# Attention and a PEER expert block on one core: the output weights prepared in the fold, the maxima of v taken over steps 76 to 118, the first projection at step 73, and three loads asked for at other places

## The chip, the cores and the metric

The kernel runs on one core of one Trainium2 chip. The metric is the device time of one launch in microseconds (us). Three runs of the kernel before took 1602.69, 1601.28 and 1598.19 us, so the median is 1601.28 us.

## The reference

A block of 2048 tokens of 448 features with two halves, each behind a layer norm and added to its input: softmax attention with 16 heads of 28 features, and a PEER layer, which picks 8 of 4096 experts per token and head through two sets of 64 sub-keys.

```python
x = A_x
h = x + _A_ref(_layernorm(x), A_wqkv, A_wo)        # 16 heads of 28 features, softmax, times wo
h2 = h + _B_ref(_layernorm(h), B_w_q, B_k1, B_k2, B_u, B_v)
...
# _B_ref, for every token and each of 16 heads
q = einsum("nd,dhc->nhc", xf, w_q)                 # 2 x 256 per head
s1 = einsum("nhd,ed->nhe", q[..., :256], k1)       # 64 scores
s2 = einsum("nhd,ed->nhe", q[..., 256:], k2)       # 64 scores
# the 8 best of each, the 8 best of their 64 sums, softmax over these: g, expert numbers top_e
act = gelu(einsum("nd,nhkd->nhk", xf, u[top_e]))
out = einsum("nhk,nhk,nhkd->nd", g, act, v[top_e])
```

## The kernel before

**Splitting.** Most products run as float16: each operand is scaled by a power of two and split into a high and a low part, so a product takes 11 or 12 matmuls of 128 rows instead of 4. The scale comes from the largest magnitude of the whole weight (class `Scale`): `see` takes the maximum of a piece on VectorE (L157), `share` takes it over all pieces (L160), spreads it (L161, tile `every`), turns it on TensorE (L165, PSUM tile `M`) and sets the scale (L178 to L181). The weights u and v are each read twice: once for the maximum (`tops`, tile `seen`, 4 buffers, 32 pieces), once to be scaled and split on GpSimd (`part`, tiles `raw` and `hl`) and written back to DRAM.

**Stages.** First the queries, keys and values of all tokens are made and written to DRAM. Then attention runs as 256 steps, and everything else of this stage is woven around it. Step u works on one of 16 groups (a block of 512 tokens and 4 heads) and on one of 16 key tiles: the scores of step u+2 (L574, tile `S`), their exponential on ScalarE (L578, tile `P`), and the values of step u (L652, PSUM tile `A`, one buffer, copied to `on` by VectorE at L659 at the end of a group). For the steps in the set `paired` the values of two steps are computed in one go. `divide` then takes the row sums through DRAM (`sum`, `rec`, `rb`) and scales `on` over the next steps (L601, L610, L611).

**The fold, steps 0 to 67.** Beside attention, the query weights of 16 heads are multiplied with the sub-keys (`Fold.run`: L280, copies `wt`, transposes L291, copies `of`), scaled and split (`Fold.parts`) and written as four weights `wp`, one for each four heads. The maxima of u are taken in steps 1 to 45.

**Steps 68 to 256.** `load_wo` loads the output weights `wo` in steps 68 to 76, takes their maximum and splits them into `woh` and `wol`. For each of the first three token blocks a projection (`project`, 26 steps: copies `oh` and `ol`, 12 matmuls with `woh` and `wol`, layer norm, transposing DMA `Xb<-hl`) starts at `begin[b]`, and a search (`search`, 33 steps) follows it: 16 score tiles of 11 matmuls with the weights `w` (L100, `M<-w,Xb`), one `fresh` tile each, and the 8 best of each 64 on VectorE (L873, L875, tile `ti`). `pairs_of` then finds the best sums (`cand`, `ts`, `pos` on VectorE, `sel` on GpSimd). The maxima of v are taken in steps 112 to 156, and v is split from step 162.

**The order.** `weave` merges the generators by due times: an entry `(generator, n, lo, hi)` gets its n turns spread evenly between steps lo and hi. Each engine executes its own instructions in exactly this order and waits in it. All DMAs are issued by SyncE (SP) from one queue in program order: where one of them must wait (for the buffer that it overwrites, or for data), all later ones wait behind it.

**The loads.** A piece of keys and values (`kS`, `V`) serves four steps; there are 4 buffers of each. At its last step the buffer is asked to be refilled with the piece four further on (L241 and L229, `load_kv`). The fold's raw weights `wr` have 8 buffers (4 heads), refilled right behind the matmuls that read them (L267). The search's tiles `w` come from one pool of 3 buffers: high and low part for one group of four heads and the high part for the next; a score tile that is the last of its group uses the low weights first.

Of the kernel before, what the change touches and what calls it, by code (L numbers as in the profile page):

```python
# [64 lines left out]
def block(ctx: ExitStack, tc: tile.TileContext, x, wqk, wv, wo, wq, k12, uT, v, cst, out):  # L65
# [120 lines left out]
    def times(dst, src, c):  # L186
        nc.vector.tensor_scalar(dst, src, c, None, op0=OP.mult)
# [19 lines left out]
    def flush():  # L207

        while due:
            due.pop(0)()  # L210
# [40 lines left out]
    class Fold:  # L251
# [18 lines left out]
        def run(self, pool, psum):  # L270

            self.folded = {}
            for h in range(H):
                yield
                flush()
                pf = psum.tile([128, 512], F32, name="M")
                w = self.raw.pop(h)
                for kt in range(2):
                    for f in range(2):
                        nc.tensor.matmul(pf[64 * f:64 * f + 64, :D], self.keys[:, f, kt], w[f][:, kt],  # L280
                                         start=kt == 0, stop=kt == 1)
                wt = pool.tile([128, 512], F32, name="wt")
                due.append(lambda: (nc.vector.tensor_copy(wt[:, :D], pf[:, :D]),
                                    nc.vector.tensor_copy(wt[:, D:], pf[:, 384:D])))
                self.load(h + 4)
                yield
                yield
                flush()
                pt = psum.tile([128, 4, 128], F32, name="M")
                for t in range(4):  # L290
                    nc.tensor.transpose(pt[:, t], wt[:, 128 * t:128 * t + 128], ident)  # L291
                of = self.folded[h] = pool.tile([128, 512], F32, name="of", bufs=8)
                due.append(lambda: (nc.vector.tensor_copy(of, pt.rearrange("p t c -> p (t c)")),
                                    WS[h // 4].see(h % 4, of)))
                yield
# [265 lines left out]
    def attention(paired):  # L561
# [84 lines left out]
        def values(u, Pt):  # L646
            n, k = divmod(u, NT)
            if k == 0:
                O[n] = P[0].tile([128, 512], F32, name="A")
            V = kv[u // 4][1]  # L650
            for j in range(4):
                nc.tensor.matmul(O[n][32 * j:32 * j + 32], V[:, k % 4, j], Pt[:, j], start=k == 0, stop=k == NT - 1)  # L652
            if k % 4 == 3:
                load_kv(u // 4 + 4)
            if k == NT - 1:
                b, g = divmod(n, 4)
                if g == 0:
                    on[b] = (w2 if b % 2 else pp).tile([128, 4, 512], F32, name="on", bufs=1)
                nc.vector.tensor_copy(on[b][:, g], O.pop(n))  # L659
# [19 lines left out]
        yield  # L679


    def load_wo():
        S = Scale("o", 4)
        raw = w2.tile([128, 4, 512], F32, name="on", bufs=1).rearrange("p g c -> p (g c)")[:, :4 * D].rearrange("p (g c) -> p g c", c=D)
        nc.sync.dma_start(raw, wo)
        yield
        yield
        for g in range(4):
            S.see(g, raw[:, g])
        yield  # L690
        yield from S.share()
        nc.vector.tensor_scalar(hscale, hscale, S.floor, 2.0 ** -TOP, op0=OP.mult, op1=OP.mult)
        for g in range(4):
            times(woh[:, g], raw[:, g], S.scale)
            nc.vector.scalar_tensor_tensor(wol[:, g], raw[:, g], S.scale, woh[:, g], op0=OP.mult, op1=OP.subtract)
            yield

    WO = 9

    X = {}  # L700

# [129 lines left out]
    def search(b, order):  # L831


        loads = {}
        heads = [i for n, (i, j) in enumerate(order) if not n or order[n - 1][0] != i]

        def load(n, k):

            if n < len(heads):
                loads[n, k] = w = sp.tile([128, 4, 4, 128], F16, name="w", bufs=3)  # L840
                nc.sync.dma_start(w, wp_d[heads[n]][:, k])

        load(0, 0)
        load(0, 1)
        load(1, 0)
        yield
        last = None
        g = 0
        for n, (i, j) in enumerate(order):
            if last:  # L850
                best(*last)
            turned = n + 1 == len(order) or order[n + 1][0] != i
            src = sp.tile([128, 512], F32, name="fresh", bufs=2)
            nc.scalar.activation(src, scores_of(*X[b], (loads[g, 0], loads[g, 1]), j, turned), AF.Identity, scale=gscale[:, i:i + 1])  # L854
# [280 lines left out]
    with tc.manual_schedule(engines={ET.PE, ET.DVE, ET.Activation, ET.Pool, ET.SP}):  # L1135
        load_kv(2)
        load_kv(3)
        begin = [FOLDED + 8, 67 + 66, 69 + 128]
        a = attention({4 * h for h in range(1, H)} | {t + k for t in begin for k in (1, 7, 13, 19)}
                      | {t + 25 + 2 * n for t in begin for n in range(16)})  # L1140
        weave((islice(a, FOLDED), FOLDED, 0, FOLDED), (fold[0].run(fold_p, P[0]), Fold.STEPS, 0, Fold.STEPS),
              *[(fold[0].parts(fold_p, i), Fold.PARTS, 16 * i + (18 if i < 3 else 16), 16 * i + 32 if i < 3 else FOLDED) for i in range(4)],
              (tops(US, lambda f: uT[:, f].rearrange("p t e -> p (t e)"), 512), TOPS, 1, 45), (US.share(), 3, 47, 50),
              (parts_of_up(0, 7), 7 + PART, 51, FOLDED))
        fp.close()
        bx = ctx.enter_context(tc.tile_pool(name="bx", bufs=1, reuse_waits="tile"))
# [12 lines left out]
        bs = ctx.enter_context(tc.tile_pool(name="bs", bufs=1, reuse_waits="tile"))  # L1159
        spare = [bs.tile([128, 512], F32, name=f"ring{i}") for i in range(16, 18)]  # L1160
        r2 = ExitStack()
        wo_p = r2.enter_context(tc.tile_pool(name="wo_p", bufs=1, reuse_waits="tile"))
        w2 = r2.enter_context(tc.tile_pool(name="w2", bufs=2, reuse_waits="tile"))
        woh = wo_p.tile([128, 4, D], F16)
        wol = wo_p.tile([128, 4, D], F16)
        work = [(a, 257 - FOLDED, 0, 257 - FOLDED), (load_wo(), WO, 0, 8)]
        for b in range(3):
            t = begin[b] - FOLDED
            look = search(b, [(i, j) for g in ((0, 1), (2, 3)) for i in range(4) for j in g])
            work += [(project(b), PROJECT, t, t + PROJECT), (islice(look, 1), 1, t + 20, t + 21)]  # L1170
            t += 26
            p = 64 * b + 174 - FOLDED
            work += [(look, SEARCH, t, t + SEARCH)]
            if b < 2:
                work += [(chain(*[pairs_of(j, nc.gpsimd) for j in range(4)]), 4 * PAIRS_POOL, t + 18, p),
                         (places_of(b, nc.scalar), PLACES, p, p + 2 * PLACES)]
            else:
                work += [(pipeline([pairs_of(j, nc.gpsimd) for j in (0, 1)], 6), 6 + PAIRS_POOL, t + 20, 257 - FOLDED)]
        w0 = weights(0)

        def first_tokens():
            load_X(0)
            yield

        work += [(islice(w0, 1), 1, 220 - FOLDED, 221 - FOLDED), (first_tokens(), 1, 234 - FOLDED, 235 - FOLDED)]
        work += [(parts_of_up(7, 32), 25 + PART, 0, 90), (tops(VS, lambda f: v[:, f], D), TOPS, 44, 88), (VS.share(), 3, 89, 92), (scales(), 1, 93, 94),
                 (parts_of_down(0, 32), 32 + PART, 94, 186)]
        weave(*work)
    att.close()
# [192 lines left out]
```

## Time and profile before

| | |
|---|---|
| median of three runs | 1601.28 us |
| the profiled execution: its time | 1600.6 us |
| its span, from the first to the last instruction | 1598.8 us |
| attention with the fold (steps 0 to 67), about | 158 to 321 us |
| attention with projections and searches (steps 68 to 256), about | 321 to 840 us |
| experts | behind that, to the end |
| DMA | 270.36 MB, mean 169 GB/s |

The profile gives, per engine, the busy time, its share of the span and the instructions; the chain of waits that ended last; groups of instructions by line; and a timeline. TensorE is PE, its weight loads are PEld, VectorE is DVE, ScalarE is ACT, GpSimd is POOL, and SPq is SyncE issuing DMAs. `x12` behind a row is the number of merged instructions, and `[7.72 <-DMA on<-in_wo_dram]` says that the engine sat idle for 7.72 us before it, until that DMA had landed. In a table of stretches each engine has its busy time with the number of instructions behind it, and the last three columns are the clock granted to TensorE, the share of the DMA engines' time and GB/s.

### The profile page before, as it was taken

Reading aid. Unit: us, or ns where it says so; the run is one execution under the profiler, and the core shown is the slowest. Engines: PE = TensorE matmul, PEld = TensorE weight load, DVE = VectorE, ACT = ScalarE, POOL = GpSimd, SP = SyncE. Lnnn points to the kernel's source line nnn. Section 1 sums busy time; section 2 is a strip of 40 time slices with the busy share of each in tenths; the row PEclk is TensorE's granted clock in tenths of the full one; section 3 lists DMA queues with packets and bytes.
Section 4 is the critical chain, followed back from the end, with each engine's and each line's share of the span. In section 5 each row is a group of like instructions: output and inputs, shape, how many; then the busy total and the mean of one; then the engine's idle time right before and its main releaser. Section 6 shows DMA issues by size and latency. Waiting matters only on the chain.

```text
span 1598.8 us, 33145 instructions
## 1 busy us (share of the span) xinstructions
PE 1528.5 (96%) x12441; PEld 646.8 (40%) x12441; DVE 1169.8 (73%) x3944; ACT 908.4 (57%) x1220; POOL 361.2 (23%) x484
## 2 busy tenths in 40 slices
PE   5999999989999999999998999999999999999998
PEld 3444222222232233222334654455445554554444
DVE  8763355554378877766598899789998998889623
ACT  3544888878788788987874432344423343333321
POOL 1242000524315754797662000000000000000000
PEclk9999999999999999999999999999999999999999
DMA  8424787557786866678733344454344534443344
GB/s 279 137 99 129 229 267 251 184 163 204 220 252 214 243 209 221 189 203 255 256 114 106 98 133 129 129 180 118 106 135 129 158 104 146 129 135 114 120 143 133
DMA packets 176042, 270.36 MB, mean 169 GB/s; under 512 B 29900, under 2 KB 105932, under 8 KB 175880
## 3 DMA queue, kind: packets, MB, share of 16 engines
q1 hardware_dynamic: 171656, 266.14, 54.1%
q10 hardware_dynamic: 4224, 2.10, 0.5%
q8 instruction: 97, 1.59, 0.4%
q14 instruction: 65, 0.53, 0.1%
HBM read 215.91 MB, written 49.50 MB: 166 GB/s over the span
## 4 chain that ended last, share of the span: by engine, by line
PE 70%; DVE 21%; DMA 3%; POOL 2%; issue 2%; ACT 1%; SPq 1%; DVEq 0%; POOLq 0%
PE acc L1290 14%; PE A L652 12%; PE M L100 12%; PE S L574 11%; PE A L100 9%; PE pq L100 6%; DVE p L1051 4%; DVE G L1072 2%; DVE fg L1036 2%; PE M L280 2%; DVE f L1030 1%; DVE ring L1262 1%; DVE pos L875 1%; PE A L1078 1%; DVE w L1265 1%
## 5 line engine op out<-in xcount | busy, mean ns | idle before, releaser
L578 ACT ACTIVATE P<-S,escale 128x1024 f32<-128x1024 f32 x512 | 533.5, 1122 | 84.8 <-PE S L574 78.9
L1290 PE MATMUL acc<-v,w 128*128 128x448 f16 x1536 | 308.3, 354 | 1.3 <-DVE w L1265 1.0
L652 PE MATMUL A<-P,V 128*32 128x512 f32 x2048 | 259.7, 605 | 2.4 <-DVE on L659 2.4
L574 PE MATMUL S<-qS,kS 32*128 32x512 f16 x3072 | 237.2, 380 | 3.0 <-ACT P L578 2.2
L1290 PEld LDWEIGHTS <-w 128*128 128x128 f16 x1536 | 148.4, 98 | 143.5 <-DVE w L1265 4.0
L100 PEld LDWEIGHTS <-u 128*128 128x128 f16 x1386 | 131.4, 98 | 147.4 <-issue 8.5
L100 PE MATMUL A<-Xb,u 128*128 128x512 f16 x759 | 178.6, 384 | 2.5 <-DVE G L1072 2.5
L100 PE MATMUL M<-w,Xb 128*128 128x512 f16 x704 | 163.8, 380 | 9.8 <-DMA w<-wp 5.0
L1216 ACT ACTIVATE ring<-A,ugelu 128x512 f32<-128x512 f32 x71 | 48.7, 687 | 217.9 <-PE A L100 217.9
L1051 DVE TENSOR_TENSOR p<-st,iota 128x2048 f16<-128x2048 f16 x128 | 156.1, 1220 | 15.7 <-PE M L1068 8.1
L574 PEld LDWEIGHTS <-kS 32*128 32x128 f16 x3072 | 65.5, 92 | 214.5 <-issue 179.0
L1262 DVE SCALAR_TENSOR_TENSOR ring<-ring,wscale,G 128x512 f32<-128x512 f32 x128 | 92.1, 745 | 77.5 <-ACT ring L1216 77.4
L100 PE MATMUL M<-Xb,u 128*128 128x512 f16 x627 | 147.8, 382 | 0.0
L100 PEld LDWEIGHTS <-Xb 128*128 128x128 f16 x704 | 63.6, 97 | 99.7 <-issue 25.9
L873 DVE MAX8 ti<-fresh 128x8 f32<-128x64 f32 x384 | 57.0, 210 | 59.7 <-ACT fresh L854 59.6
L1264 ACT ACTIVATE w<-ring 128x512 f16<-128x512 f32 x128 | 75.9, 622 | 41.1 <-DVE ring L1262 28.6
L652 PEld LDWEIGHTS A<-P,V 128*32 128x32 f32 x2048 | 47.9, 109 | 126.2 <-issue 114.2
L1108 POOL TENSOR_SCALAR raw<-raw,scale 128x512 f32<-128x512 f32 (+1 forms) x64 | 47.2, 737 | 209.6 <-DVE r L601 145.4
L1265 DVE SCALAR_TENSOR_TENSOR w<-w,ring 128x512 f16<-128x512 f16 x128 | 84.9, 685 | 7.2 <-ACT w L1264 6.9
L1216 ACT ACTIVATE ring<-M,ugelu 128x512 f32<-128x512 f32 x57 | 39.2, 688 | 89.2 <-PE M L100 87.5
L1036 DVE TENSOR_TENSOR fg<-f,st 128x2048 f16<-128x2048 f16 x64 | 77.8, 1215 | 0.1
L875 DVE FIND_INDEX8 ti<-ti,fresh 128x8 uint32<-128x64 f32 x384 | 76.8, 218 | 0.0
(209 smaller groups left out, 1882.1 us busy)
## 6 DMA issues: line engine op xcount, KB each, us to landing
v<-vs SPq DMA_DIRECT2D x128, 336.0 KB, 2.9
u<-us SPq DMA_DIRECT2D x126, 256.0 KB, 2.6
w<-wp SPq DMA_DIRECT2D x56, 512.0 KB, 5.4
kS<-ks SPq DMA_DIRECT2D x64, 256.0 KB, 4.8
V<-vd SPq DMA_DIRECT2D x64, 256.0 KB, 3.3
wr<-in_wq_dram SPq DMA_DIRECT2D x32, 448.0 KB, 3.5
vs<-hl SPq DMA_DIRECT2D x32, 336.0 KB, 5.6
seen<-in_uT_dram SPq DMA_DIRECT2D x32, 256.0 KB, 4.6
```

Of the source, the lines that this page charges most:

```text
L100: nc.tensor.matmul(ps, l, r, start=i == 0, stop=i == len(pairs) - 1)
L574: nc.tensor.matmul(S[j // 2][:, j % 2], kS[r, a, 128 * (k % 4):128 * (k % 4) + 128], qS[r, c], start=m == 0, stop=m == 2)
L578: nc.scalar.activation(Pt[:, 2 * i:2 * i + 2], S[i], AF.Exp, scale=escale[:, n % 4:n % 4 + 1])
L652: nc.tensor.matmul(O[n][32 * j:32 * j + 32], V[:, k % 4, j], Pt[:, j], start=k == 0, stop=k == NT - 1)
L875: nc.vector.max_index(i, t, src)
L1036: nc.vector.tensor_tensor(fg.rearrange("p t k f u -> p t k (f u)"), f1.rearrange("p t f u -> p t (f u)").unsqueeze(2).to_broadcast([128, T ...
L1051: newest[0] = nc.vector.tensor_tensor(p1, pairs(0, s, TG, 128), ids(TG, 128), op=OP.is_equal).ins
L1216: gelu[0] = nc.scalar.activation(act, p, AF.Gelu_apprx_tanh, scale=ugelu).ins
L1262: nc.vector.scalar_tensor_tensor(av, av, wscale, of_expert(b, f), op0=OP.mult, op1=OP.mult)
L1264: nc.scalar.activation(w[:, 0], a, AF.Copy, scale=1.0 / LS)
L1265: newest[0] = nc.vector.scalar_tensor_tensor(w[:, 1], w[:, 0], -LS, a, op0=OP.mult, op1=OP.add).ins
L1290: nc.tensor.matmul(acc[j][:, :D], l, r, start=f == 0 and k == 0, stop=f == 31 and k == 2)
```

## The change

Six edits, all in the attention stage:

1. `wo` is loaded as four DMAs into the four `seen` buffers at step 51, inside the fold; its maximum and scale follow until step 58 (`scale_wo`). What is left at steps 69 to 73 is the split into `woh` and `wol` (`split_wo`).
2. The maxima of v are taken in steps 76 to 118 and no longer in 112 to 156.
3. The first projection starts at step 73 (was 76), and with it the first search, 99 (was 102), and their paired steps; the other two stay.
4. The search's high weights get a pool of 2 buffers and its low weights one of their own.
5. Keys and values: a piece is asked for at the second step of a piece, three pieces ahead, into the buffer whose last reader ran two steps earlier.
6. The fold's raw weights are asked for two steps later.

```diff
@@ class Fold, run
+                yield
+                yield
                 self.load(h + 4)
-                yield
-                yield
                 flush()
@@ values(u, Pt)
-            if k % 4 == 3:
-                load_kv(u // 4 + 4)
+            if k % 4 == 1 and u > 4:
+                load_kv(u // 4 + 3)
@@ load_wo becomes scale_wo and split_wo
-        raw = w2.tile([128, 4, 512], F32, name="on", bufs=1).rearrange("p g c -> p (g c)")[:, :4 * D].rearrange("p (g c) -> p g c", c=D)
-        nc.sync.dma_start(raw, wo)
...
+    def scale_wo():
         for g in range(4):
+            wor.append(sp.tile([128, 512], F32, name="seen", bufs=4)[:, :D])
+            nc.sync.dma_start(wor[g], wo[:, g])
+        yield
+        yield
+        for g in range(4):
+            WO.see(g, wor[g])
+            if g % 2:
+                yield
+        yield from WO.share()
+        nc.vector.tensor_scalar(hscale, hscale, WO.floor, 2.0 ** -TOP, op0=OP.mult, op1=OP.mult)
+        yield
+
+    def split_wo():
+        for g in range(4):
+            times(woh[:, g], wor[g], WO.scale)
+            nc.vector.scalar_tensor_tensor(wol[:, g], wor[g], WO.scale, woh[:, g], op0=OP.mult, op1=OP.subtract)
+            yield
@@ search(b, order)
-                loads[n, k] = w = sp.tile([128, 4, 4, 128], F16, name="w", bufs=3)
+                loads[n, k] = w = sp.tile([128, 4, 4, 128], F16, name="w", tag="w" + "hl"[k], bufs=2 - k)
@@ the weaves
-        begin = [FOLDED + 8, 67 + 66, 69 + 128]
+        begin = [FOLDED + 5, 67 + 66, 69 + 128]
...
-              (parts_of_up(0, 7), 7 + PART, 51, FOLDED))
+              (scale_wo(), 7, 51, 58), (parts_of_up(0, 7), 7 + PART, 51, FOLDED))
...
-        work = [(a, 257 - FOLDED, 0, 257 - FOLDED), (load_wo(), WO, 0, 8)]
+        work = [(a, 257 - FOLDED, 0, 257 - FOLDED), (split_wo(), 4, 1, 5)]
...
-                 ..., (tops(VS, lambda f: v[:, f], D), TOPS, 44, 88), ...
+                 ..., (tops(VS, lambda f: v[:, f], D), TOPS, 8, 50), ...
```

Three places show how the instructions move. **VectorE at the start of step 68's stage, before**: `topso` is the maximum of `wo`, read from `on` (the buffer that `wo` was loaded into); `rb` and `on` on the rows between belong to attention's division.

```order
L157 TENSOR_REDUCE topso<-on 128x1 x4
L610 RECIPROCAL rb<-rb 128x128
L611 SCALAR_TENSOR_TENSOR on<-on,onscale,rb 128x128
L160 TENSOR_REDUCE topo<-topso 128x1
L161 COPY every<-topo 128x128
L610 RECIPROCAL rb<-rb 128x128
L611 SCALAR_TENSOR_TENSOR on<-on,onscale,rb 128x128
L178 TENSOR_REDUCE topo<-M 128x1
L179 TENSOR_SCALAR topo<-topo 128x1
```

In the changed kernel these maxima stand in the fold, on VectorE at steps 53 to 56, between the fold's copies `wt` and `of` (the piece of the difference):

```order
 L601 RECIPROCAL r<-r 128x16
+L157 TENSOR_REDUCE topso<-seen 128x1 x2
 L283 COPY wt<-M 128x448
 L284 COPY wt<-M 128x64
+L157 TENSOR_REDUCE topso<-seen 128x1 x2
 L187 TENSOR_SCALAR hlf<-of,scalew_230 128x512
 L307 SCALAR_TENSOR_TENSOR hlf<-of,scalew_230,hlf 128x512
+L160 TENSOR_REDUCE topo<-topso 128x1
+L161 COPY every<-topo 128x128
 L293 COPY of<-M 128x512
```

So the wait for `wo` has moved from step 69 to step 53, and the DMA that it waits for from step 68 to step 51.

**SP's queue at the first search, before**, from the keys of the search's first steps to the weights of the second group of heads (`wp_67` its low ones, `wp_68` the high ones of the group after it). `xd<-Xb` stores the projected block and waits for its transposing DMAs; `rb<-rec` is attention's division.

```order
L229 DMA kS<-ks_64 128x2x512
L241 DMA V<-vd 128x512
L772 DMA xd_86<-Xb 128x2048
L773 DMA xd_86<-Xb 128x1536
L1115 DMA us_104<-hl 128x1024
L1103 DMA raw<-in_uT_dram 128x512
L592 DMA rb<-rec_175 32x512 x4
L841 DMA w<-wp_67 128x2048
L841 DMA w<-wp_68 128x2048
```

The same place in the changed kernel:

```order
L229 DMA kS<-ks_64 128x2x512
L241 DMA V<-vd 128x512
L777 DMA xd_86<-Xb 128x2048
L778 DMA xd_86<-Xb 128x1536
L1120 DMA us_103<-hl 128x1024
L1108 DMA raw<-in_uT_dram 128x512
L1099 DMA seen<-in_v_dram 128x448
L846 DMA w<-wp_67 128x2048
L846 DMA w<-wp_68 128x2048
```

The four `rb<-rec` stand behind the weights now, one load of v stands in their place, and the `V` at the top overwrites a buffer whose reader ran two steps before.

**VectorE at the start of the second projection (step 133), before**, up to the first `oh`; 33 more rows follow before the second tile's `oh`, five more `tops` among them:

```order
L610 RECIPROCAL rb<-rb 128x128
L611 SCALAR_TENSOR_TENSOR on<-on,onscale,rb 128x128
L873 MAX ti_29326<-fresh 128x8 x4
L875 MAX_INDEX ti_29326<-ti_29326,fresh 128x8 x4
L157 TENSOR_REDUCE tops_215<-seen 128x1
L610 RECIPROCAL rb<-rb 128x128
L611 SCALAR_TENSOR_TENSOR on<-on,onscale,rb 128x128
L873 MAX ti_29427<-fresh 128x8 x4
L875 MAX_INDEX ti_29427<-ti_29427,fresh 128x8 x4
L106 CAST oh_30004<-on 128x512
L721 TENSOR_TENSOR ol_30005<-on,oh_30004 128x512
```

and in the changed kernel, where 22 more rows follow before the second tile's `oh`:

```order
L610 RECIPROCAL rb<-rb 128x128
L611 SCALAR_TENSOR_TENSOR on<-on,onscale,rb 128x128
L878 MAX ts_27551<-cand 128x8 x4
L880 MAX_INDEX pos<-ts_27551,cand 128x8 x4
L610 RECIPROCAL rb<-rb 128x128
L611 SCALAR_TENSOR_TENSOR on<-on,onscale,rb 128x128
L106 CAST oh_30079<-on 128x512
L726 TENSOR_TENSOR ol_30080<-on,oh_30079 128x512
```

The maxima `tops` of v and the last groups of the search (`ti`) have left this place; what stays are the division, the sums of pairs (`ts`, `pos`) and the projection itself.

More of the change, by code (lines that the diff above doesn't have):

```diff
@@ L284, in run @@
                                     nc.vector.tensor_copy(wt[:, D:], pf[:, 384:D])))
-                self.load(h + 4)
                 yield
                 yield
+                self.load(h + 4)
                 flush()
@@ L679, in attention @@
         yield
-    def load_wo():
-        S = Scale("o", 4)
-        raw = w2.tile([128, 4, 512], F32, name="on", bufs=1).rearrange("p g c -> p (g c)")[:, :4 * D].rearrange("p (g c) -> p g c", c=D)
-        nc.sync.dma_start(raw, wo)
+    WO = Scale("o", 4)
+    wor = []
+    def scale_wo():
+        for g in range(4):
+            wor.append(sp.tile([128, 512], F32, name="seen", bufs=4)[:, :D])
+            nc.sync.dma_start(wor[g], wo[:, g])
         yield
@@ L688, in load_wo @@
         for g in range(4):
-            S.see(g, raw[:, g])
+            WO.see(g, wor[g])
[3 more added lines that the diff above has]
+        nc.vector.tensor_scalar(hscale, hscale, WO.floor, 2.0 ** -TOP, op0=OP.mult, op1=OP.mult)
         yield
-        yield from S.share()
-        nc.vector.tensor_scalar(hscale, hscale, S.floor, 2.0 ** -TOP, op0=OP.mult, op1=OP.mult)
+    def split_wo():
         for g in range(4):
-            times(woh[:, g], raw[:, g], S.scale)
-            nc.vector.scalar_tensor_tensor(wol[:, g], raw[:, g], S.scale, woh[:, g], op0=OP.mult, op1=OP.subtract)
+            times(woh[:, g], wor[g], WO.scale)
+            nc.vector.scalar_tensor_tensor(wol[:, g], wor[g], WO.scale, woh[:, g], op0=OP.mult, op1=OP.subtract)
             yield
-    WO = 9
     X = {}
@@ L1185, in block @@
         work += [(islice(w0, 1), 1, 220 - FOLDED, 221 - FOLDED), (first_tokens(), 1, 234 - FOLDED, 235 - FOLDED)]
-        work += [(parts_of_up(7, 32), 25 + PART, 0, 90), (tops(VS, lambda f: v[:, f], D), TOPS, 44, 88), (VS.share(), 3, 89, 92), (scales(), 1, 93, 94),
+        work += [(parts_of_up(7, 32), 25 + PART, 0, 90), (tops(VS, lambda f: v[:, f], D), TOPS, 8, 50), (VS.share(), 3, 89, 92), (scales(), 1, 93, 94),
                  (parts_of_down(0, 32), 32 + PART, 94, 186)]
```

## The prediction

> **What bounds the kernel now.** The page comes first, for the engine that the chain of waits runs through (shares of the span).
>
> ```profile
> PE 70%; DVE 21%; DMA 3%; POOL 2%; issue 2%; ACT 1%; SPq 1%; DVEq 0%; POOLq 0%
> ```
>
> TensorE carries 70% of the chain. The change adds no product and removes none, so it can only win where TensorE stood still. Where that is, the table of stretches says (us, then the busy time of PE, PEld, DVE, ACT, POOL; last the granted clock, the DMA share and GB/s).
>
> ```profile
> 320.00:360.00 40.00, 32.84 (x313) 8.21 (x313) 21.29 (x44) 29.80 (x31) 9.60 (x12) 0.91 0.52 164
> 360.00:400.00 40.00, 39.16 (x371) 10.80 (x374) 17.22 (x31) 34.19 (x35) 16.32 (x21) 1.00 0.71 205
> 400.00:440.00 40.00, 37.08 (x336) 11.03 (x334) 15.47 (x120) 31.55 (x32) 14.05 (x17) 1.00 0.70 217
> ```
>
> In these three stretches, which hold the change's first steps, TensorE stands still for 7.2, 0.8 and 2.9 us. Its list of waits names what ended such gaps (total us, times, longest), and SP's list what its queue stood behind:
>
> ```profile
> PE M L165 <- DVE every L161: 7.5, 2, 7.2
> PE M L100 <- DMA w<-wp: 5.0, 2, 2.9
> PE M L100 <- DVE oh L106: 3.3, 2, 2.2
> PE A L652 <- DVE on L659: 2.4, 3, 0.8
> SPq L241 <- PE A L652: 121.1, 48, 5.6
> ```
>
> **The change part by part.** *wo in the fold.* The timeline around 326 us:
>
> ```profile
> 324.16 1.08 PE L574 MATMUL S<-qS,kS 32*128 32x512 f16 x12
> 326.17 1.08 PE L574 MATMUL S<-qS,kS 32*128 32x512 f16 x12
> 331.25 2.20 DVE L157 TENSOR_REDUCE topso<-on 128x1 f32<-128x448 f32 x4 [7.72 <-DMA on<-in_wo_dram]
> 335.41 0.48 PE L165 MATMUL M<-ct,every 128*128 128x128 f32 x1 [7.16 <-DVE every L161]
> 343.05 1.08 PE L574 MATMUL S<-qS,kS 32*128 32x512 f16 x12
> ```
>
> VectorE waits for the load of wo, TensorE waits for VectorE, and runs on at a lower clock (0.91 over the stretch from 320 us). Normal steps are 2.01 us apart (324.16 to 326.17). From 326.17 to 343.05 there are four steps (the others start at 335.82, 339.08 and 340.96): 16.88 us where 8.04 were due, a loss of 8.84. All of that goes if wo's scale is there at step 69. What comes back is the turned tile inside the fold, where TensorE is the bound and no wait on it shows:
>
> ```profile
> 276.20 0.33 PE L165 MATMUL M<-ct,every 128*128 128x128 f32 x1
> ```
>
> That is 0.33 us. Four maxima (2.20 us in the row above) and their small operations come to VectorE in the fold, and the four loads are asked for two steps ahead, 4.8 us at the fold's 2.4 us a step (163 us for 68). By the order rows SP reaches them behind `r<-sum`, and since the keys before them no longer wait for TensorE, earlier than before. If they were late all the same, VectorE's copies `wt` and `of` would stand behind `topso`, and TensorE behind those; that is a rival below. The split stays behind the fold, in steps 69 to 73, and VectorE reaches it without that wait. Net: -8.5.
>
> *The first search's second weights.* The low weights of the second group were late:
>
> ```profile
> 411.68 0.32 SPq L241 DMA_DIRECT2D V<-vd  x1
> 417.25 5.52 DMA w<-wp
> 419.02 1.68 PE L100 MATMUL M<-w,Xb 128*128 128x512 f16 x7
> 427.14 2.55 PE L100 MATMUL M<-w,Xb 128*128 128x512 f16 x11
> ```
>
> SP stood before `V` until TensorE had ended the old piece (411.68), then issued eight DMAs in a row, the four `rb<-rec` among them, and reached the weights at 417.25. TensorE was through the seven high products at 420.7. The tiles are 8.12 us apart where 5.85 is the rule (next fence): 2.27 lost. In the changed order `V` waits for nothing late and the four `rb` stand behind the weights, so SP can ask as soon as the low weights are free, after four products of the tile before, near 414.2. The landing took 5.52 us, so they arrive near 419.7. I take the full -2.27. The separate buffer for the low part adds nothing that I can see: the low part already was read first and freed first.
>
> *Paired steps moved by three.* 95, 111 and 127 were in the paired set, and each is the last step of a group: the second step of the pair needs the one tile `A`, which VectorE first has to copy out.
>
> ```profile
> 427.21 2.48 PE M L100 x11
> 433.06 2.48 PE M L100 x11
> 437.37 0.70 DVE on L659
> 439.94 2.48 PE M L100 x11
> ```
>
> In this chain two search tiles are 5.85 us apart, and 6.88 where the copy lies between: 1.03 for each of the three (the waits give 2.4 us in 3 times; the rest is the pairing that is lost). The new first steps of pairs in this block are all even, so no pair lies across two groups: -3.1.
>
> *The second projection.* At step 139 TensorE waited for VectorE:
>
> ```profile
> 348.15 1.85 PE A L652 x16
> 350.76 2.38 PE M L100 x12
> 518.59 1.92 PE L652 MATMUL A<-P,V 128*32 128x512 f32 x16
> 498.65 0.96 DVE rb L610
> 503.15 0.51 DVE ti L873 x4
> 503.66 0.79 DVE ti L875 x4
> 521.45 0.53 DVE tops L157
> 523.03 0.42 DVE L106 CAST oh<-on 128x512 f16<-128x512 f32 x1
> 523.50 4.13 PE M L100 x12
> 524.00:528.00 4.00, 4.00 (x19) 1.56 (x21) 1.91 (x4) 0.00 (x0) 3.85 (x6) 0.61 1.08 311
> ```
>
> In the first projection the products follow the values by 2.61 us and take 2.38; here by 4.91 and 4.13, at a clock of 0.61: 4.05 lost. The chain there is VectorE's own work from the arrival of `rb` at 498.65 to 523.03. Out of these 24.4 us the change takes six `tops` (0.53 each) and three groups of `ti` (0.51 + 0.79 each): 7.1 us. The products were 2.3 late, so that is covered three times over; `oh` is ready near 516 and TensorE is next, at 521.2. Net -4.05. The Trainium skill, page "TensorE: Matmul & The Clock Gate", section "What's actually happening", has the array at half clock only after an idle window of about 3.4 us; this gap was 2.2 us and the row shows 0.61 all the same, so the row decides. By the page 1.75 of the 4.05 would not belong to the gap, and the sum below would be 1.8 us smaller.
>
> *The maxima of v in steps 76 to 118.* Their 32 loads of 224 KB now meet the first projection. One load in 1.2 steps (2.8 us) is about 80 GB/s, so the stretch of 360 to 400 us would go from 205 to some 285 GB/s and its share from 0.71 towards 0.95. VectorE has room (17 of 40 us). How loads fare beside such traffic:
>
> ```profile
> seen<-in_v_dram SPq DMA_DIRECT2D x22, 224.0 KB, 3.8
> w<-wp SPq DMA_DIRECT2D x9, 512.0 KB, 4.6
> w<-wp SPq DMA_DIRECT2D x3, 512.0 KB, 8.0
> ```
>
> The first two rows are of 440 to 520 us, search and maxima together, and no wait of TensorE on `w` falls there; the last is of 520 to 560, projection and maxima together, and there the weights took 8.0 us. Asked for at 414.2 they would land at 422.2 at that rate, 1.5 us late. I bound the cost by 0 and by what the third search loses to the same wait (below): 4.7. I take 0, the row of search with maxima.
>
> *Keys and raw weights later.* The keys are asked for 9 steps before their first scores instead of 11, at 2.0 us or more a step 18 us, against 8.0 for the slowest load above. The raw weights have 14 steps. The fold has no wait of TensorE on either, so I take 0. What SP gains, 121.1 us of waits, is no time of its own; it only makes other transfers earlier. It does not help the third search:
>
> ```profile
> 741.95 0.32 SPq L772 DMA_DIRECT2D xd<-Xb  x1
> 745.72 5.67 DMA w<-wp
> 741.09 2.49 PE M L100 x11
> 757.45 2.48 PE M L100 x11
> ```
>
> There SP stands before `xd`, that is before the landing of the last transposing DMA, until 741.95, and reaches the weights at 745.72. Two tiles take 16.36 us instead of 11.70: 4.66 lost. The changed order has two key loads more ahead of `xd`, inside SP's wait. I take 0, between -4.7 (the wait goes) and +1.4 (two more issues at the 0.7 us that each of eight took from 411.68 to 417.25).
>
> Sum: -8.84 + 0.33 - 2.27 - 3.06 - 4.05 = -17.9 us. The profiled execution took 1600.6 us, 0.7 below the median of the three runs; against the median the forecast is 1601.3 - 17.9 = 1583.4 us.
>
> **The rivals.** *The weights of the first search stay late* because the maxima of v crowd the DMA engines: the gain of 2.27 goes and the loss grows to the third search's 4.66, together 4.7 us worse, 1588.1. For it speaks the 8.0 us row, against it SP's earlier request. The Trainium skill, "DMA: Bandwidth & Descriptors", section "Latency and other measured facts", gives HBM access 0.2 us on average and 2 us under high load, which would put the weights near 421.5; the two landing rows (4.6 and 8.0 us) agree that load costs microseconds.
>
> *The third search is cured too*, as its last keys no longer stand in SP's way before the transposing DMA: 1583.4 - 4.7 = 1578.7. Against it: that DMA waited for VectorE, and behind it for GpSimd.
>
> *The second projection still waits* (another row of VectorE waits for a DMA in its place): 1583.4 + 4.05 = 1587.5.
>
> *The change does not do what it says for wo*: the loads come late in the fold, VectorE stands, and TensorE waits for `wt`. Its price is at most the whole 8.84: 1592.2. Against it: from the issue at step 51 to the turned tile at step 56 it is five steps, 12 us, and the whole load, in one piece, kept VectorE for 7.72 in the row above.
>
> *Slower: the keys come late.* SP's queue now holds 32 more loads behind VectorE between steps 76 and 118, and a piece must land within 18 us of its place. If SP lags by more than 10 us (18 less 8.0), every later piece makes TensorE wait. It would take 0.5 us on each of some 60 pieces to turn -17.9 into +12, 1613. SP's longest wait behind `V` was 5.6 us, so this is far off, and only lasting crowding would do it.
>
> **How the numbers follow.** Forecast 1583.4: 0.50. First search late, 1588.1: 0.17. Third search cured, 1578.7: 0.15. Second projection waits, 1587.5: 0.06. wo late, 1592.2: 0.07. Keys late, 1613: 0.03. Several mishaps that meet near no change: 0.02. The range reaches from the cure with the spread of the runs, 1577, to the case of wo, 1593. Faster by over 0.3% (4.8 us, about what a measurement of this kernel can tell from no change) are all but the last two: 0.95, same 0.02, slower 0.03.
>
> **What would show it.** In the changed profile TensorE's waits should have no L165 above 0.4 us and no wait on `on` L659 in pairs; steps near 335 us should be 2.0 us apart with a clock of 1.00. Near 405 to 410 us the search tiles should be 5.85 apart from the first. Near 505 us the second `oh` should end before the values of its step, with no dip of the clock. The stretch of the first projection should show a DMA share near 0.95 and no TensorE gap. The forecast is wrong if TensorE waits for `w` at the first search, for `kS` or `V` anywhere, or if the fold, about 163 us long, grows by more than half a microsecond.

## The result, and the profile after

The changed kernel took 1583.71 us (median of 4 runs, 1578.99 to 1589.57) beside 1601.29 us of the kernel before on the same chip: a ratio of 0.9895, 95% interval 0.9854 to 0.9935. A second series of six runs had a median of 1583.01 us, ratio 0.9900 (0.9878 to 0.9922). The forecast was 1583.4 us.

First the same stretches as before (PE, PEld, DVE, ACT, POOL; clock, DMA share, GB/s), of the first profile of the changed kernel:

```profile
320.00:360.00 40.00, 40.00 (x394) 10.61 (x384) 27.29 (x49) 36.84 (x37) 11.27 (x16) 1.00 0.69 207
360.00:400.00 40.00, 39.78 (x380) 11.07 (x379) 20.32 (x51) 35.55 (x36) 16.66 (x22) 1.00 1.05 295
400.00:440.00 40.00, 39.40 (x345) 12.58 (x341) 24.62 (x172) 32.66 (x35) 11.99 (x16) 1.00 0.92 301
```

Where TensorE stood still for 7.2, 0.8 and 2.9 us, it stands for 0, 0.2 and 0.6. The clock of the first stretch is 1.00, not 0.91, and the maxima of v show as a DMA share of 1.05. Its waits, and SP's before `V`:

```profile
PE M L100 <- DMA w<-wp: 3.9, 2, 3.3
PE M L100 <- DVE oh L106: 1.6, 2, 1.0
PE M L280 <- DVE topo L178: 0.5, 1, 0.5
PE M L165 <- DVE every L161: 0.3, 1, 0.3
SPq L241 <- PE A L652: 54.9, 31, 5.1
```

The wait for wo (7.2 of the 7.5 us before) is gone: the 0.3 us left on L165 belong to the scale of the fold's weights, a wait of 0.34 us in both kernels. That on `on` (2.4 in 3) is gone too. Of the wait on `oh`, the second projection's part fell from 2.23 to 0.58 us; the third projection's 1.03 us are as before. The wait on `w` is still 3.9, 0.60 at the first search and 3.27 at the third, and a new one of 0.5 stands in the fold.

The whole time hides part of this, since both ends of the program vary from run to run. **A yardstick** that varies far less: the stretch from the first product of the fold to the first product of the third search, which runs at the same step in both kernels. In the timeline of TensorE, before:

```profile
163.04 1.72 PE L280 MATMUL M<-wr,kr 128*64 128x448 f32 x8
735.17 2.55 PE L100 MATMUL M<-w,Xb 128*128 128x512 f16 x11
```

and after:

```profile
165.54 1.72 PE L280 MATMUL M<-wr,kr 128*64 128x448 f32 x8
721.70 2.55 PE L100 MATMUL M<-w,Xb 128*128 128x512 f16 x11
```

572.13 us before, 556.16 after: 15.97 less. A second profile of the changed kernel, of an execution that took 1581.73 us, gave 721.64 - 165.44 = 556.20. So two executions 7.8 us apart agree here within 0.04 us; 0.1 us of their difference lies ahead of the fold, the rest behind this point. In part that agreement is chance: the second execution lost 0.45 us more at the first search and 0.5 less in the fold. Two profiles of the kernel with the later stores (below) are 0.36 us apart, so I take half a microsecond as what the stretch can tell. The experiments are read by this stretch, by the stalls in it, and only then by their medians:

| kernel | median, us (runs) | ratio to before, interval | stretch, us | lost in first search | lost in third search |
|---|---|---|---|---|---|
| before | 1601.29 (4) | | 572.13 | 2.27 | 4.66 |
| after | 1583.71 (4) | 0.9895 (0.9854 to 0.9935) | 556.16 | 0.77 | 4.98 |
| after, again | 1583.01 (6) | 0.9900 (0.9878 to 0.9922) | 556.20 | 1.22 | 3.88 |
| wo alone | 1591.00 (10) | 0.9946 (0.9929 to 0.9963) | 565.22 | 3.62 | 5.92 |
| pairs alone | 1615.43 (4) | 1.0098 (1.0070 to 1.0125) | 588.14 | no wait on `w`, tiles 7.17 apart | 1.96 |
| maxima back | 1584.04 (4) | 0.9905 (0.9880 to 0.9930) | 558.18 | 0 | 1.14 |
| step back | 1583.77 (4) | 0.9903 (0.9880 to 0.9926) | 561.03 | 0.77 | 1.31 |
| both back | 1589.71 (5) | 0.9945 (0.9926 to 0.9963) | 562.63 | 0 | 1.52 |
| keys back | 1587.93 (4) | 0.9932 (0.9908 to 0.9955) | 558.07 | 2.98 | 2.71 |
| small parts back | 1582.67 (4) | 0.9892 (0.9870 to 0.9914) | 556.32 | 1.24 | 1.68 |
| later stores | 1578.60 (5) | 0.9871 (0.9849 to 0.9893) | 555.69 | 0.25 | 0 |
| later stores, again | 1578.04 (5) | 0.9862 (0.9838 to 0.9886) | 556.05 | 0 | 0 |
| later stores, step back | 1581.82 (6) | 0.9890 (0.9869 to 0.9911) | 559.61 | 0 | 0 |

"Lost" is what the two tiles around the wait take beyond 11.70 us; what the third search loses comes behind the stretch. Each ratio is to runs of the kernel before in the same series.

### The profile page after: what moved, and what is told of

It reads as the page before. It is cut to its first block, busy times and chain, and to the rows that moved or that the text cites. A ratio compares the mean times of both kernels' runs of the same rounds, so it can differ in the third digit from the quotient of the medians.

```text
span 1587.8 us, 33145 instructions
## 1 busy us (share of the span) xinstructions
PE 1528.4 (96%) x12441; PEld 647.1 (41%) x12441; DVE 1168.6 (74%) x3944; ACT 907.6 (57%) x1220; POOL 360.4 (23%) x484
## 4 chain that ended last, share of the span: by engine, by line
PE 70%; DVE 22%; DMA 3%; POOL 2%; issue 2%; ACT 1%; SPq 0%; DVEq 0%; POOLq 0%; ACTq 0%
PE acc L1295 13%; PE A L652 13%; PE M L100 12%; PE S L574 11%; PE A L100 9%; PE pq L100 6%; DVE p L1056 4%; DVE G L1077 2%; DVE fg L1041 2%; PE M L280 2%; DVE ring L1267 1%; DVE pos L880 1%; DVE w L1270 1%; DVE f L1035 1%; PE A L1083 1%
```

## The experiments

### wo alone

The kernel before with edit 1 alone.

```diff
-        raw = w2.tile([128, 4, 512], F32, name="on", bufs=1)...
-        nc.sync.dma_start(raw, wo)
+            wor.append(sp.tile([128, 512], F32, name="seen", bufs=4)[:, :D])
+            nc.sync.dma_start(wor[g], wo[:, g])
...
+              (scale_wo(), 7, 51, 58), (parts_of_up(0, 7), 7 + PART, 51, FOLDED))
...
-        work = [(a, 257 - FOLDED, 0, 257 - FOLDED), (load_wo(), WO, 0, 8)]
+        work = [(a, 257 - FOLDED, 0, 257 - FOLDED), (split_wo(), 4, 1, 5)]
```

> The kernel before with one edit: wo is loaded and its scale found in the fold (steps 51 to 58), the split stays behind it (steps 69 to 73); the first projection stays at step 76. Theory A (the stall of TensorE behind VectorE's maxima of wo is a loss of its own, and nothing else was hidden behind it): the 7.2 us wait of M L165 goes, the four steps from 326 us on take 8.0 us instead of 16.9, the turned tile comes back as 0.3 to 0.7 us in the fold: 8.2 to 8.5 us less, near 1592.9 us. Rival B (VectorE and the DMA queue are what is late there, and the next thing that needs them, the first projection at step 76, then waits instead): the gain is half or less, 1597 us or more, with a new wait of TensorE on VectorE or on a load before 360 us.

1591.0 us; by the ratio 8.6 below the kernel before. The wait for wo is gone. The timeline of TensorE at the first search and at the second projection:

```profile
416.99 1.02 PE L100 MATMUL M<-w,Xb 128*128 128x512 f16 x4 [3.45 <-DMA w<-wp]
517.70 1.47 PE L100 MATMUL M<-woh,oh 128*128 128x448 f16 x4 [2.25 <-DVE oh L106]
```

The stretch is 6.91 us shorter, where -8.84 + 0.33 = -8.51 was forecast. The missing 1.6 us stand in the rows: the first search's weights are 3.45 late (2.11 before), so that 3.62 are lost there instead of 2.27, and the fold waits 0.2 us on `topo`. A is right on the stall itself and B on a fifth of it: once VectorE's wait is gone, TensorE is through with the seven high products 8.3 us earlier, counted from the start of the fold, and the weights are there only 6.9 us earlier.

### pairs alone

```diff
-                      | {t + 25 + 2 * n for t in begin for n in range(16)})
+                      | {t + 25 - (t == begin[0]) + 2 * n for t in begin for n in range(16)})
```

> The kernel before with one edit: the 16 paired steps of the first search begin one step earlier (even steps instead of odd ones), so that two of the three pairs that lay across two groups (111 and 127) do so no more; the third (95, a paired step of the projection) stays. Theory A (a pair across two groups costs 1.03 us, 6.88 us instead of 5.85 between two search tiles, and nothing takes its place): TensorE's wait A L652 on `on` L659 falls from 2.4 us in 3 times to about 0.8 in 1, and the time by 2.1 us, to 1599.2 us, which a run of three rounds can only just tell from none; the trace's wait decides. Rival B (the copy of the old sums is late whatever the pairing is, so that the wait moves to the next step): the waits of A L652 stay near 2.4 us in all, and the time at 1601.3 us.

14.4 us slower than the kernel before; neither theory had that. TensorE's waits:

```profile
PE S L574 <- ACT P L578: 18.6, 19, 1.1
PE A L652 <- DVE on L659: 0.8, 1, 0.8
```

The wait on `on` fell to 0.8 in 1, as A said. But the paired steps had also been shifted against the search's products, which stayed where they were. The chain of waits of this kernel, start and length:

```profile
419.20 2.48 PE M L100 x11
421.68 0.81 PE S L574 x12
422.49 0.04 issue
422.53 1.12 ACT P L578
423.65 0.04 issue
423.70 0.82 PE S L574 x10
424.52 1.85 PE A L652 x16
426.37 2.48 PE M L100 x11
```

Two groups of scores now stand next to each other, and the second needs ScalarE to have read the first (1.12 us). Tiles are 7.17 us apart, not 5.85. In the changed kernel the pairs moved together with the products (scores, product, scores, values of two steps). So this run measures the price of a wrong phase and not that of a pair across two groups; the kernels with the step put back measure that.

### The maxima back, the step back, and both

```diff
-        ... (tops(VS, lambda f: v[:, f], D), TOPS, 8, 50), ...
+        ... (tops(VS, lambda f: v[:, f], D), TOPS, 44, 88), ...
```

> The changed kernel with one part undone: the maxima of v stand in steps 112 to 156 again, the first projection stays at step 73. Theory A (each stall is paid where VectorE or a load is late, and the earlier projection alone, three steps or some 6 us, covers the 2.3 us by which the second projection's products were late): no wait of M L100 on oh over 0.5 us near 511 to 526 us; the first search's weights have less beside them and its first two tiles take 11.7 instead of 12.5 us: 0.8 us less than the changed kernel, near 1583 us. Rival B (it is the maxima of v on VectorE that make the second projection late, as the prediction's count of 3.2 us of them says): the wait on oh comes back, with a granted clock near 0.6 behind it, 2 to 4 us more than the changed kernel, 1586 to 1588 us.

```diff
-        begin = [FOLDED + 5, 67 + 66, 69 + 128]
+        begin = [FOLDED + 8, 67 + 66, 69 + 128]
```

> The changed kernel with one part undone: the first projection begins at step 76 again, the maxima of v stay in steps 77 to 119, so that the paired steps of the first search keep their place to its products and are odd again. Theory A (a pair that lies across two groups costs 1.03 us, and there are three; the second projection is freed by the maxima of v that are gone from VectorE there): TensorE's waits of A L652 on `on` L659 are 2.4 us in 3 times again, the second projection waits 1 us or less, as in the changed kernel: 3.1 us more, 1586.8 us. Rival B (it is the three steps of lead of the first projection that free the second one): besides, the wait of M L100 on oh near 510 to 530 us is 2 us or more, with a lower clock behind it: 5 to 7 us more in all, 1589 to 1591 us.

Both edits together:

> The changed kernel with both undone: first projection at step 76, maxima of v in steps 112 to 156; wo stays in the fold, the keys and the low weights as changed. Theory A (the second projection's stall needs both: VectorE then has three groups of `ti` and six maxima more to do before its `oh`): the second products come 2 us late or more with the clock near 0.6 behind them, 4 us lost there, and 3.1 us by the three pairs: 7 us more than the changed kernel, 1590.8 us, less what the third search gains where it waits less (up to 4 us, as it did with the maxima alone put back). Rival B (the maxima alone make the stall, as they brought a wait of 4.1 us in 3 times when they were put back alone): the same wait as then, near 4 us with the clock at 1.00, and only the pairs on top: 3.1 us more than that kernel.

The timeline of TensorE at the second projection, with the maxima back:

```profile
511.34 0.93 PE L100 MATMUL M<-woh,oh 128*128 128x448 f16 x4 [1.37 <-DVE oh L106]
526.90 0.93 PE L100 MATMUL M<-woh,oh 128*128 128x448 f16 x4 [1.63 <-DVE oh L106]
```

and with both back:

```profile
514.73 1.67 PE L100 MATMUL M<-woh,oh 128*128 128x448 f16 x4 [3.49 <-DVE oh L106]
516.20 1.70 PE L100 MATMUL M<-wol,oh 128*128 128x448 f16 x4
```

Three waits of 0.89, 0.42 and 0.37 us (1.68 in all) stand there with the step alone back, 3.00 with the maxima alone, and 3.49 with slow products behind it (1.67 instead of 0.93 us for four) with both. The changed kernel keeps 0.58. So each edit takes part of VectorE's lateness, and only both together come near zero. With the maxima alone back, B was right that the wait returns, but not on the low clock (0.93 us for four products is full speed) nor on the time; A was right that the first search then waits for nothing. With the step alone back, A was right on the waits on `on`, 2.4 us in 3; the second projection's 1.68 us lie between the two theories, and the median of 1583.8 us is below both. With both back, A was right that the low clock returns, and the median of 1589.7 us lies between the 1590.8 that it gave and the 4 us less that it allowed for the third search.

In the stretch the step is worth 4.87 us (561.03 - 556.16): three pairs at 1.03 and some 1.1 in the second projection. Most of the other 0.7 is one wait on `oh` in the third projection, 1.64 us instead of 1.03; two executions of the kernel with the later stores differ there as well (1.10 and 1.64), so it is not shown to be the step's. The maxima are worth 2.02: 2.4 gained at the second projection, 0.77 paid at the first search, where with the maxima back no tile is late; 0.4 is left unnamed. The two medians hardly show it (1583.8 and 1584.0 us). In the profiles of these kernels the third search, behind the stretch, lost only 1.1 to 1.3 us, against 3.9 and 5.0 in the changed kernel, which offsets much of it.

### Keys back, small parts back

```diff
-            if k % 4 == 1 and u > 4:
-                load_kv(u // 4 + 3)
+            if k % 4 == 3:
+                load_kv(u // 4 + 4)
```

> The changed kernel with one part undone: keys and values are asked for as before, at the last step of a piece. Theory A (SP's queue then stands before `V` until TensorE has ended the old piece, and the first search's second weights stand behind it): SP's wait L241 on A L652 is near 120 us again, the request for `w` leaves later, and the first search's first two tiles take 13.5 to 14.6 us instead of 12.5: 1 to 2 us more than the changed kernel, 1585 to 1586 us. Rival B (`xd`, which waits for the transposing DMA, is what holds SP there, and `V` is free by then): the first two tiles take 12.5 us as in the changed kernel, the time stays at 1583.7 us.

```diff
+                self.load(h + 4)
                 yield
                 yield
-                self.load(h + 4)
...
-                loads[n, k] = w = sp.tile([128, 4, 4, 128], F16, name="w", tag="w" + "hl"[k], bufs=2 - k)
+                loads[n, k] = w = sp.tile([128, 4, 4, 128], F16, name="w", bufs=3)
```

> The changed kernel with its two small parts undone: the low weights of the search share one buffer of three with the high ones again, the raw weights of the fold are asked for two steps earlier. Theory A (the low part was read and freed first anyway, and the raw weights were in time anyway): no wait of TensorE changes by 0.5 us, the time stays at 1583.7 us. Rival B (the separate buffer is what lets the second group's low weights be asked for early): the request for `w` near 403 us leaves 2 us later or more and the first search's first two tiles take 14 us or more instead of 12.5: 1585.5 us or more.

SP's queue with the keys back, start and length of each issue:

```profile
392.20 0.33 SPq L241 DMA_DIRECT2D V<-vd  x1
392.75 2.04 SPq L761 DMA_TRANSPOSE Xb<-hl  x1
...
398.95 0.32 SPq L777 DMA_DIRECT2D xd<-Xb  x1
...
402.29 0.96 SPq L846 DMA_DIRECT2D w<-wp  x2
```

and what TensorE makes of it:

```profile
408.30 1.02 PE L100 MATMUL M<-w,Xb 128*128 128x512 f16 x4 [2.82 <-DMA w<-wp]
```

SP's wait before `V` is 135.9 us again. But `V` is not what holds the weights directly: behind it stands the transposing DMA, behind that the stores `xd`, which wait for it to land, and only then `w`. Counted from the start of the fold, `xd` leaves 2.1 us later than in the changed kernel (235.9 against 233.8) and the weights 1.9 later. The first search loses 2.98 us instead of 0.77, and the stretch grows by 1.91. A, with one link more. By the ratios the time rose by 5 to 6 us, with intervals that overlap those of the changed kernel; the third search lost less than there, so what goes beyond the 1.9 us is not explained by what I measured.

With the small parts back the stretch is 0.16 us longer. The first search then waits twice (0.45 and 0.46 us) and not once (0.60). They are worth nothing that can be measured.

### The changed kernel again, later stores, and the step put back in it

Every kernel so far reaches `w` behind `xd`, at the first and at the third search. The stores of a block were put behind the requests:

```diff
-        if not room:
-            store_X(b)
...
                 load(g + 1, 1)
                 load(g + 2, 0)
+                if g == 0:
+                    store_X(b)
```

> The changed kernel with one edit: SP issues the stores `xd` of a block (which wait for the landing of the transposing DMA) behind the search's first requests for weights of the second group instead of ahead of them. Theory A (the weights are late because SP's queue stands before `xd`: order of the queue): in the third search the request for `w` leaves SP some 4 to 5 us earlier, its first two tiles take 11.7 us instead of 16.7, the first search's two take 11.7 instead of 12.5: 5.0 + 0.8 us less than the changed kernel, near 1578 us. Rival B (the weights are late because the transfer itself is slow there, 6.5 us for 512 KB beside the other loads, or because the buffer that they fill comes free late): the request leaves earlier or as before but TensorE's wait M L100 on w stays above 3 us in all, and the time stays near 1583.7 us.

> The changed kernel itself once more, with a profile of its own and five rounds, beside the kernel with the later stores. Theory A (the first profile, the slowest of its four runs, shows waits of a poor run: the third search's weights came 3.3 us late there, where kernels with the same code around that place waited 1.0 to 1.7 us): the third search's two tiles take 13 us instead of 16.7, the first search's 12.5 as before, the median is near 1582 us. Rival B (the poor landing belongs to this kernel, by where its transfers fall): the third search takes 16.4 us or more again, the median is near 1584 us or above.

> The kernel with the later stores once more, in the same call as the changed kernel, to compare the two on one chip. Theory A (the order of SP's queue is what the third search loses, 1.1 to 5.0 us by the run, and 0.5 us of the first): no wait of TensorE on w over 0.5 us in either, and a median 2 to 5 us below that of the changed kernel. Rival B (the gain of the first comparison was the luck of the runs): a median within 1 us of the changed kernel's.

SP's queue and TensorE at the third search in the changed kernel (first tile at 721.70):

```profile
728.30 0.33 SPq L777 DMA_DIRECT2D xd<-Xb  x1
...
731.77 1.90 SPq L846 DMA_DIRECT2D w<-wp  x2
```

```profile
738.36 1.86 PE L100 MATMUL M<-w,Xb 128*128 128x512 f16 x4 [3.27 <-DMA w<-wp]
```

and SP's queue with the later stores (second profile, first tile at 722.19):

```profile
727.54 0.55 SPq L586 DMA_DIRECT2D sum<-on  x1
729.11 1.83 SPq L844 DMA_DIRECT2D w<-wp  x2
730.99 0.43 SPq L775 DMA_DIRECT2D xd<-Xb  x1
```

The request leaves 6.9 us behind the first tile instead of 10.1, and TensorE waits for no `w` there any more, in two profiles. The kernel gains 5.0 us on the changed one in the same series (1578.04 against 1583.01 us). At the two searches 3.9 and 1.2 us that the changed kernel's second profile lost come back, the 3.9 behind the stretch. The stretch itself is only 0.1 to 0.5 us shorter: in the second profile of the later stores the fold waits 0.4 us and the third projection 0.6 us more than in that of the changed kernel. This kernel is the fastest of the table. A stands: the order of SP's queue. The changed kernel's own repetition lay between its theories, with 3.88 lost: its weights are late in both profiles, by 3.27 and 2.08 us.

> The kernel with the later stores, and the first projection at step 76 again, so that no wait on w hides the difference. Theory A (three pairs across two groups cost 1.03 us each, and the second projection waits some 1.1 us more, as it did with the step alone put back): 3 to 4.2 us more than the kernel with the later stores, near 1582 us, with the waits on `on` L659 at 2.4 us in 3 times. Rival B (the step of the first projection is worth nothing, since the kernel with it put back took 1583.8 us, as the changed one): within 1 us of the kernel with the later stores.

1581.82 us, 3.8 above the kernel with the later stores; the stretch is 3.6 to 3.9 longer and the waits on `on` are 2.4 us in 3. Without the noise of the late weights the step has the price that A gave.

## Why the prediction was right

**wo in the fold, -8.84 +0.33.** Right. Steps near 335 us are 2.01 apart at full clock. The fold pays a little more, 0.77 us from its first product to its last (143.55 us, 142.78 before). Its chain in the first profile:

```profile
296.32 0.69 DVE topsw L157
297.01 0.82 DVE hlf L187
297.85 1.53 DVE hlf L307
299.38 0.21 DVE topo L178
299.60 0.04 issue
299.64 1.72 PE M L280 x8
```

In the timeline TensorE reaches this product 10.23 us after the one before it (at 289.41), where 9.45 is the rule without the turned tile: 0.78 instead of 0.33. VectorE answers the turned tile (`topo`) only behind the split of the fold's own weights, the two `hlf`, and TensorE's tile `M` is held until then. I had counted only the tile itself. In the second profile that wait is not there, and the fold pays 0.28.

**First search, -2.27.** Mis-sized: 1.50 and 1.05 came. I had named `V` and the four `rb` as what holds SP. They went, but `xd` remained: SP stood before it from 397.86 to 399.29 and issued five DMAs before `w`. I had seen that in the third search and not looked for it in the first. The 0.77 that is missing needs both that order and the maxima beside it, which I had taken at 0: nothing is lost with the maxima back, and 0.25 and 0 with the stores later. The rival of 4.7 us was the right mechanism at a fifth of its size.

**Paired steps, -3.06.** Right: the waits on `on` are gone, and return, 2.4 us in 3, with the step put back.

**Second projection, -4.05.** About 3.5 came. The cause, VectorE's work, was right; the slack was not. I had counted 7.1 us less on VectorE and `oh` ready some 5 us ahead of TensorE. The chain at the third tile:

```profile
520.92 0.56 POOL rstd L120
521.51 0.86 DVE xn L123
...
524.10 1.10 DVE hl L137
525.21 0.47 DVE oh L106
525.72 2.44 PE M L100 x12
```

The layer norm of the first tile (`xn`, four `hl`, 3.7 us together) stands ahead of this `oh` on VectorE and waits for GpSimd (`rstd`). GpSimd's timeline has this row directly ahead of `rstd`:

```profile
517.19 3.36 POOL L939 TENSOR_TENSOR sel<-sel 128x1024 f16<-128x1024 f16 x2
```

The input of `rstd` (`mv`, on VectorE) was ready at 515.27, so GpSimd was behind with the work of the search before. So 0.58 us is lost one tile later than I had counted: the rival of a wait that takes the place of the old one, at a seventh of its price, and with GpSimd's own work in the place of the DMA that the rival named.

**Third search, 0.** Right for the changed kernel (4.98 and 3.88, before 4.66). The later stores show that the named cause, SP before `xd`, is the cause. The kernels with a part put back lose only 1.1 to 2.7 with the same code there. With the maxima back the wait is 0.98 us instead of 3.27: `xd` leaves 5.3 us behind the first tile instead of 6.6, the request for `w` 9.1 instead of 10.1, and `w` lands in 5.20 us instead of 6.55. So a slower transfer has a share of more than half in that difference, and why it is slower was not settled.

**Separate low buffer and raw weights, 0.** Right (0.16). **Keys, 0 in themselves.** Right as a price; the part of the first search that came is theirs, 1.9 to 2.2 us.

**The sum.** -17.9 forecast, -15.97 in the stretch. The 1.9 missing are 0.77 (first search), 0.58 (second projection), about 0.45 (fold) and 0.1. By the ratios the whole time fell by 16.8 and 16.0 us, with intervals of 10.4 to 23.4 and 12.5 to 19.5; the medians are 17.6 and 18.7 us apart. So it is not shown that anything was gained outside the stretch, where two executions of the changed kernel differ by 7.8 us. The sum of the terms was met to about 10%; that the median met the forecast to 0.3 us is luck.

Two of the signs that the prediction had named for being wrong did appear: TensorE waits for `w` at the first search (0.60 and 1.06 us), and the fold grew by more than half a microsecond in one of the two profiles (0.77 and 0.28). Both are small beside the sum, and they are the terms named above.

## What to carry to other kernels

When a load is late, follow the one queue back past the instruction that waits longest: behind the wait that you remove stands the next (`V`, then the transposing DMA, then the store that waits for its landing), and a request moved ahead of all of them cost nothing here. Slack on an engine is not the work taken away from it: count to the next instruction that waits for another engine, one tile further on too. Measure an edit by a stretch between two instructions that both kernels execute at the same step, and move paired steps only together with the work that lies between them.

## What the runs showed of the hardware

TensorE's clock after a pause is not set by the pause's length alone. The two profiles of the kernel with the later stores, the same program, from 160 to 200 us; first the one, then the other:

```profile
160.00:200.00 40.00, 40.00 (x386) 10.92 (x384) 15.45 (x28) 35.08 (x35) 0.00 (x0) 1.00 0.75 242
```

```profile
160.00:200.00 40.00, 39.87 (x363) 10.26 (x362) 12.49 (x23) 33.37 (x33) 0.00 (x0) 0.93 0.69 223
```

The clock is 1.00 in one and 0.93 in the other, and the fold begins at 163.03 and 166.14 us. Of these 3.1 us, 0.86 lie ahead of attention's first scores (155.24 and 156.10); the other 2.25 are the clock, 1.00 in one and 0.50 in the other from 160 to 163 us. No pause of TensorE there is longer than 0.99 us in either. Stalls behave alike: behind a wait of 2.08 us for `w` at 737.11 the clock was 0.78 in one profile of the changed kernel, and behind one of 2.55 us at 737.08 it was 1.00 with the keys back:

```profile
736.00:740.00 4.00, 2.89 (x20) 0.77 (x23) 1.11 (x11) 1.20 (x2) 1.06 (x2) 0.78 0.99 339
```

```profile
736.00:740.00 4.00, 2.92 (x28) 0.93 (x31) 1.14 (x11) 1.73 (x3) 0.91 (x2) 1.00 0.96 312
```

Over all profiles, seven of the eleven waits above 2 us for `w` and `oh` in the searches and projections were followed by the low clock, and none of the shorter ones (up to 1.88 us). The Trainium skill, "TensorE: Matmul & The Clock Gate", section "What's actually happening", has a free-running window of about 3.4 us, so that the point of transition depends on where in the window the work falls. The same program at 0.50 and at 1.00 would fit that. That a pause must fill 3.4 us does not: 2.08 us was enough, and 3.45 us (wo alone, first search) was followed by a clock of 1.00.
